# First MLP in six tiles of 512 tokens, with a layer's operands in one part of the memory and the first tile's first two steps in 384 and 128 columns

## The chip, the cores and the metric

The kernel runs on one core of one Trainium2 chip. The metric is the device time of one execution in microseconds, the median of several runs. TensorE (PE in the profile) multiplies, VectorE (DVE) and ScalarE (ACT) work on the results, GpSimd (POOL) is nearly unused, and SyncE (SP) issues the transfers.

## The reference

Attention over chunks of 32 tokens, each with 16 tokens of context on its left and 8 on its right and 8 memory keys, for 4 batches, 8 heads and 768 tokens of head size 64, is followed by two MLPs on the 3,072 tokens of 512 features it yields:

```
for c in range(seq // 32):
    k_full = concat([mem_k, k[max(0, c*32-16) : min(S, c*32+40)]])
    a = exp(s - max(s)) / (sum + 1e-9)      # s = scale * q_c @ k_full.T
    out[c] = a @ v_full
...
h = x @ w_in                                # 512 -> 2048
g = where(h > 0, h, exp(min(h, 0)) - 1)
x = g @ w_out                               # 2048 -> 512
...
h = x @ w_in2
g = s * relu(h)**2 + b
return g @ w_out2                           # 512 features
```

All is fp32. The kernel splits each operand of the MLPs into a high and a low part (fp32r) and makes three matmuls for one product: high x high, high x low, low x high.

## The kernel before, in words

*Attention* goes by 24 units of 128 tokens (six for each batch). A unit has its scores (`psS`, or `psVS` when they share a step with the values of the unit before), a softmax on DVE and ACT (`softmax`, L222 to L237; the first and last unit of a batch also add a mask, L228), transposes of the weights (`step_P`), and the values (`values`, L278, into `psV` or `psVS`). In the units below `NU0` the transposes are four matmuls (`psP`, L251) and a copy on ACT; in the others they are 16 short transposes on DVE (`pt<-sm`, L258). The result of a unit goes straight into `xh` and `xl` for the first two tiles and otherwise by way of DRAM (`x_dram`), from where `load_x` fetches a tile.

*The first MLP* goes by tiles of tokens (`sizes`, eight of three units, 384 tokens) and in each by 16 chunks of 128 hidden features. A step `h1` multiplies a chunk (12 matmuls into `psH`: four blocks of 128 features, three products each; L326 to L328) and makes the activation: two steps on ACT, a sum on DVE (L352), then the high part on ACT and the low one on DVE (`gl`, L184). The step `out1` for the same chunk comes two steps later and adds 12 matmuls into four accumulators `acc`. After a tile's last chunk `put_out` copies the accumulators (L376, L380, L382) into `big`, which goes to `y_dram`.

*The order.* Tile 0's first six chunks come first, then all of tile 1, then the rest of tile 0, then tiles 2 to 7 in order (`seq`). `mlp1_step` gives each half step a share of the attention's remaining steps (`beside`) and of the weights' splitting (`weights_to`; `w<-t`, `t<-raw` on DVE and ACT); the attention is spread over tiles 2, 3 and 4 and ends at tile `TATT` = 5. From there, until tile 7's chunk 8, `prepared` spreads the 160 steps that prepare the second MLP's weights. From tile 7's chunk 10, `load_blocks` fetches what the second MLP starts with. A scheduler decides from that list how each engine's instructions stand, each by its dependences and their priority.

*The second MLP* multiplies blocks of 512 columns in seven products in place of eight (`first_layer`, `second_layer`; `psH<-xc,ws`, `psL<-g2h,ws`), 2,016 matmuls of 512 columns each, with its weight pieces `ws` fetched from DRAM.

*The memory.* Weights of the first MLP lie in two pools, chunks 0 to 7 in one on the right, the others on the left; pools for the second MLP (`xcp`, `wsp`, `yrp`, `ghp`) open on the right where the first eight chunks were, once tile 7 has reached chunk 10 and the pools are closed.

Of the kernel before, what the change touches and what calls it, by code (L numbers as in the profile page):

```python
# [28 lines left out]
NU0 = 6  # L29
HF = 6  # L30
TATT = 5
NFREE = 8
MICRO = 8
HN, NT2 = 512, 3
ORDER = (1, 2, 6, 5, 7, 3, 4)
# [18 lines left out]
def tile_attention_then_two_mlps(ctx, tc, q_in, k_in, v_in, w1, w2, s_in, b_in, out):  # L54
# [22 lines left out]
    def engine(step):  # L77
# [5 lines left out]
    sizes = [3] * 8  # L83
# [8 lines left out]
    early = [ExitStack(), ExitStack()]  # L92
# [10 lines left out]
    ps_v = vctx.enter_context(tc.tile_pool(name="ps_v", bufs=1, space=PSUM))  # L103
    ps_acc = []
# [37 lines left out]
    def split_w(c, i, raw):  # L142

        t = wst.tile([P, DM], I32, tag="t", name="t")
        yield from to_f32(raw, t)
        nm = "io"[i]
        parts = wps[c >= NFREE].tile([P, 2, DM], F32R, tag=f"w{i}_{c}", name=f"w{i}_{c}")
# [183 lines left out]

    def h_mm(t, c, n, xx):
        ps = ps_h.tile([P, 512], F32, tag="h", name="psH")
        for kk in range(KT):
            mm3(ps[:, :n], W["i", c], xx, lambda a: a[:, kk * P:(kk + 1) * P], lambda a: a[:, kk, :n],
                kk == 0, kk == KT - 1)
        return ps
# [20 lines left out]
    def accumulators(t):  # L358
        if not ps_acc:
            vctx.close()  # L360
            ps_acc.append(pctx.enter_context(tc.tile_pool(name="ps_acc", bufs=1, space=PSUM)))
        ACC[t] = [ps_acc[0].tile([P, 512], F32, tag=f"acc{m}", name=f"acc{m}") for m in range(KT)]

    def put_out(t, c, n):
# [6 lines left out]
        if c == NF - 1 or c == HF - 1 and split:  # L371
            for m, acc in enumerate(ACC[t]):
                with tc.high_priority(400):
# [3 lines left out]
                    else:  # L377
                        o = big_tile(n, t >= TATT and m > 0 or m == 3 and t >= 2)
# [145 lines left out]
    ws, used = [], [0]  # L524

    def load_pieces(n):

        while len(ws) < min(n, len(pieces)):
            lay, ii, jj = pieces[len(ws)]
            w = p2["wsp"].tile([P, 2, 2 * P], F32R, tag="ws", name="ws")  # L530
# [12 lines left out]
    def load_blocks(t):  # L543

        t0 = t * 2 * HN
        xc = XC[t] = {j: p2["xcp"].tile([P, 2, 2, HN], F32R, tag=f"xc{j}", name=f"xc{j}") for j in ORDER}
        b12 = p2["yrp"].tile([P, 2, HN], F32, tag="yr", name="b12")
        b11, b21, b22 = (f(xc[j][:, 1]) for j in (1, 2, 3))
# [4 lines left out]
        t3, t2, t4 = (p2["yrp"].tile([P, 2, HN], F32, tag="yr", name=nm) for nm in ("t3", "t2", "t4"))  # L553
# [4 lines left out]
        for j in ORDER:  # L558
            nc.scalar.activation(out=xc[j][:, 0], in_=src[j], func=AF.Copy)
            sub(xc[j][:, 1], src[j], xc[j][:, 0])  # L560
            yield

    def open_second():

        for nm, k, c in (("xcp", 1, ctx), ("wsp", 12, ctx), ("yrp", 4, early[1])):
            p2[nm] = c.enter_context(tc.tile_pool(name=nm, bufs=k, side="right", reuse_waits="tile"))
        p2["blocks"] = load_blocks(0)

    def mlp1_step(t, c):
# [18 lines left out]
        if c == 0 and t == TATT:  # L588
            actx.close()
            op.append(mctx.enter_context(tc.tile_pool(name="op2", bufs=2)))  # L590
            p2["prep"] = early[1].enter_context(tc.tile_pool(name="prep", bufs=2, side="right", reuse_waits="tile"))
# [15 lines left out]
        if t == NTILE1 - 1 and c >= NFREE + 2:  # L607
# [6 lines left out]
    def prepared(t, n):  # L614

        want = min(NPREP * (2 * NF * (t - TATT) + n) // (2 * NF * (NTILE1 - TATT) - 2 * (NF - NFREE)), NPREP)
        while t >= TATT and p2["n"] < want:
# [13 lines left out]
    for slot in seq[-2:]:  # L631
# [6 lines left out]
    early[1].close()  # L638
    g2p, evp, outp, p2["yrp"] = (
        ctx.enter_context(tc.tile_pool(name=nm, bufs=k, reuse_waits="tile"))  # L640
        for nm, k in (("g2p", 4), ("evp", 5), ("outp", 4), ("yrp2", 4)))
    ghp = ctx.enter_context(tc.tile_pool(name="ghp", bufs=3, side="right", reuse_waits="tile"))
# [16 lines left out]
    def first_layer(t, i, g):  # L659

        xc, ii, acc = XC[t], i % 2, {}
        for j in ORDER:
# [4 lines left out]
            for k in range(2):  # L667
                mm3(o, (w[:, 0], w[:, 1]), (xc[j][:, 0], xc[j][:, 1]), lambda a: a[:, k * P:(k + 1) * P],
# [26 lines left out]
    def second_layer(t, gs, beside):  # L695

        keep, acc = {}, {}
        for j in ORDER:
# [4 lines left out]
            for q, g in enumerate(gs):  # L703
                gl, gh = (ghp.tile([P, 2, HN], F32R, tag=nm, name=nm) for nm in ("g2l", "g2h"))
# [99 lines left out]
```

## Time and profile before

| what | value |
|---|---|
| runs | 1091.55, 1089.6, 1096.9 us; median 1091.55 |
| profiled execution, its time and its span | 1094.46 us, 1092.7 us |
| TensorE busy | 1072.1 us (98%), 8,206 matmuls |
| VectorE busy | 783.6 us (72%), 1,299 instructions |
| ScalarE busy | 592.1 us (54%), 939 instructions |
| chain that ended last | PE 82%, DVE 8%, DMA 5%, ACT 3% |
| mean TensorE clock granted | 0.99 |

"Busy" is the time in which at least one instruction of an engine runs; the matmuls overlap, so that a row's mean duration is longer than the distance between two starts. The pace of a run of matmuls is the distance of two starts divided by the number of matmuls between them. In a table of windows the number after x counts the instructions in a window, PEclk is the granted TensorE clock (1.00 is 2.4 GHz, 0.50 is 1.2 GHz), and the DMA share is the mean over the 16 engines.

### The profile page before, as it was taken

Reading aid. Unit: us, or ns where it says so; the run is one execution under the profiler, and the core shown is the slowest. Engines: PE = TensorE matmul, PEld = TensorE weight load, DVE = VectorE, ACT = ScalarE, POOL = GpSimd, SP = SyncE. Lnnn points to the kernel's source line nnn. Section 1 sums busy time; section 2 is a strip of 40 time slices with the busy share of each in tenths; the row PEclk is TensorE's granted clock in tenths of the full one; section 3 lists DMA queues with packets and bytes.
Section 4 is the critical chain, followed back from the end, with each engine's and each line's share of the span. In section 5 each row is a group of like instructions: output and inputs, shape, how many; then the busy total and the mean of one; then the engine's idle time right before and its main releaser. Section 6 shows DMA issues by size and latency. Waiting matters only on the chain.

```text
span 1092.7 us, 20633 instructions
## 1 busy us (share of the span) xinstructions
PE 1072.1 (98%) x8206; PEld 966.0 (88%) x8206; DVE 783.6 (72%) x1299; ACT 592.1 (54%) x939; POOL 0.7 (0%) x6
## 2 busy tenths in 40 slices
PE   7999999999999999999999999999999999999998
PEld 5889999999999999999999987788888788888887
DVE  6899846778678777998884655697356696365854
ACT  4888444334434446787784455754355644255542
POOL 0000000000000000000000000000000000000000
PEclk7899999999999999999999999999999999999999
DMA  8955032433524315898886266777766777766673
GB/s 307 373 221 220 1 109 88 153 102 105 174 81 145 125 40 173 319 335 298 331 326 236 90 187 191 244 210 231 230 191 185 231 214 225 212 197 191 200 204 127
DMA packets 98113, 213.70 MB, mean 196 GB/s; under 512 B 9952, under 2 KB 27360, under 8 KB 95968
## 3 DMA queue, kind: packets, MB, share of 16 engines
q1 hardware_dynamic: 97440, 211.59, 59.4%
q8 instruction: 65, 1.06, 0.4%
q10 hardware_dynamic: 576, 0.79, 0.2%
q14 instruction: 32, 0.26, 0.1%
HBM read 164.89 MB, written 47.45 MB: 194 GB/s over the span
## 4 chain that ended last, share of the span: by engine, by line
PE 82%; DVE 8%; DMA 5%; ACT 3%; issue 1%; SPq 0%; ACTq 0%; DVEq 0%
PE psH L326 14%; PE psH L328 13%; PE psH L327 13%; PE psL L327 7%; PE acc L326 6%; PE psL L328 6%; PE acc L327 6%; PE acc L328 6%; PE psL L326 6%; DVE pt L258 2%; DMA xc<-y_dram 2%; DMA xl<-x_dram 1%; DMA x_dram<-xs 1%; PE psVS L278 1%; PE psVS L219 1%
## 5 line engine op out<-in xcount | busy, mean ns | idle before, releaser
L326 PE MATMUL psH<-xh,w 128*128 128x384 f32 x512 | 175.4, 343 | 2.6 <-ACT pt L180 1.1
L326 PE MATMUL acc<-gh,w 128*128 128x384 f32 x512 | 173.0, 339 | 0.9 <-DVE big L376 0.8
L328 PE MATMUL psH<-xh,w 128*128 128x384 f32 x512 | 173.6, 339 | 0.0
L327 PE MATMUL psH<-xl,w 128*128 128x384 f32 x512 | 173.2, 338 | 0.2 <-DVE xl L184 0.2
L327 PE MATMUL acc<-gl,w 128*128 128x384 f32 x512 | 171.9, 336 | 0.0
L328 PE MATMUL acc<-gh,w 128*128 128x384 f32 x512 | 171.9, 336 | 0.0
L705 ACT ACTIVATE g2h<-g 128x1024 fp32r<-128x1024 f32 x84 | 89.2, 1062 | 89.9 <-PE psL L328 89.6
L327 PE MATMUL psL<-g2l,ws 128*128 128x512 f32 x336 | 131.0, 390 | 1.6 <-DVE g2l L184 1.6
L326 PE MATMUL psH<-xc,ws 128*128 128x512 f32 x336 | 131.8, 397 | 0.6 <-ACT p L656 0.6
L328 PE MATMUL psH<-xc,ws 128*128 128x512 f32 x336 | 131.1, 390 | 0.0
L326 PE MATMUL psL<-g2h,ws 128*128 128x512 f32 x336 | 130.4, 389 | 0.6 <-ACT g2h L705 0.6
L327 PE MATMUL psH<-xc,ws 128*128 128x512 f32 x336 | 130.9, 390 | 0.0
L328 PE MATMUL psL<-g2h,ws 128*128 128x512 f32 x336 | 130.7, 389 | 0.0
L184 DVE TENSOR_TENSOR g2l<-g,g2h 128x1024 fp32r<-128x1024 f32 x84 | 102.2, 1222 | 39.5 <-ACT g2h L705 39.2
L350 ACT ACTIVATE g<-psH 128x384 f32<-128x384 f32 x128 | 62.5, 488 | 113.1 <-PE psH L328 67.0
L180 ACT ACTIVATE gh<-g 128x384 fp32r<-128x384 f32 x128 | 66.9, 522 | 86.8 <-DVE g L352 85.6
L352 DVE SCALAR_TENSOR_TENSOR g<-g,psH 128x384 f32<-128x384 f32 x128 | 70.5, 551 | 49.3 <-ACT g L351 48.4
L326 PEld LDWEIGHTS psH<-xh,w 128*128 128x128 f32 x512 | 97.0, 189 | 5.2 <-ACT pt L180 1.4
L326 PEld LDWEIGHTS acc<-gh,w 128*128 128x128 f32 x512 | 96.6, 189 | 2.4 <-DVE big L376 1.1
L327 PEld LDWEIGHTS psH<-xl,w 128*128 128x128 f32 x512 | 97.1, 190 | 0.5 <-DVE xl L184 0.4
L328 PEld LDWEIGHTS psH<-xh,w 128*128 128x128 f32 x512 | 97.2, 190 | 0.2
L327 PEld LDWEIGHTS acc<-gl,w 128*128 128x128 f32 x512 | 96.2, 188 | 0.3 <-DVE gl L184 0.2
(97 smaller groups left out, 1668.1 us busy)
## 6 DMA issues: line engine op xcount, KB each, us to landing
ws<-s_dram SPq DMA_DIRECT2D x336, 256.0 KB, 2.9
raw<-w SPq DMA_DIRECT2D x64, 512.0 KB, 5.4
s_dram<-right SPq DMA_DIRECT2D x16, 1024.0 KB, 4.5
kb<-k SPq DMA_DIRECT2D x24, 512.0 KB, 5.6
v<-v SPq DMA_DIRECT2D x24, 512.0 KB, 4.3
s_dram<-left SPq DMA_DIRECT2D x16, 768.0 KB, 3.6
q<-q SPq DMA_DIRECT2D x24, 256.0 KB, 5.5
out<-r SPq DMA_DIRECT2D x24, 256.0 KB, 3.5
```

What stands on the lines that cost most here:

```text
L180: return nc.scalar.activation(out=hi, in_=src, func=AF.Copy)
L184: return nc.vector.tensor_tensor(out=lo, in0=src, in1=f(hi), op=ALU.subtract)
L219: mm = nc.tensor.matmul(ps[o, z, r * NCK:(r + 1) * NCK], q[rows, r * U + c * CH:r * U + (c + 1) * CH], kb[rows, r, c * NCK:(c + 1) * NCK], ...
L258: nc.vector.transpose(out=pt[k * CH:(k + 1) * CH, :, rows], in_=sm[rows, :, z, n0:n0 + CH])
L278: nc.tensor.matmul(ps[r % 2 * D:(r % 2 + 1) * D, z, o:o + CH], v[rows, (r * NC + c) * D:(r * NC + c + 1) * D], pt[rows, r, cs], start=True ...
L326: nc.tensor.matmul(o, sa(a[0]), sb(b[0]), start=first, stop=False, skip_group_check=again)
L327: nc.tensor.matmul(o, sa(a[0]), sb(b[1]), start=False, stop=False, skip_group_check=again)
L328: return nc.tensor.matmul(o, sa(a[1]), sb(b[0]), start=False, stop=last, skip_group_check=again)
L350: nc.scalar.activation(out=g[:, :n], in_=ps[:, :n], func=AF.Relu, scale=-1.0)
L352: nc.vector.scalar_tensor_tensor(out=g[:, :n], in0=g[:, :n], scalar=-1.0, in1=ps[:, :n], op0=ALU.add, op1=ALU.max)
L705: nc.scalar.activation(out=gh, in_=g[:, block], func=AF.Copy)
```

## The change

The tiles have four units, 512 tokens, six in all. The first two tiles take eight units, so `NU0` is 8. Chunks 0 and 1 of tile 0 are multiplied in two parts: in 384 columns (`psE`) as soon as three units (`NEARLY`) are done and in 128 columns after the fourth. The attention's last step comes at `ATT_END`, tile 3, chunk 8; the second MLP's weights are prepared from there on until the last tile's chunk 10. The weights of the first layer of the first MLP and the tiles `xh`, `xl` lie on the right; later their memory holds the weight pieces, the blocks `xc` and the parts `g2h`, `g2l` of the second MLP. Those of the second layer lie on the left.

```
-    sizes = [3] * 8
+    sizes = [4] * 6
-NU0 = 6
-TATT = 5
-NFREE = 8
+NU0 = 8
+NEARLY = 3
+ATT_END = (3, 8)
+NBLOCK = 10
...
-    wps = [early[0].enter_context(tc.tile_pool(name="wpa", bufs=1, side="right")),
-           mctx.enter_context(tc.tile_pool(name="wpb", bufs=1))]
+    wps = [ctx.enter_context(tc.tile_pool(name="wpi", bufs=1, side="right")),
+           mctx.enter_context(tc.tile_pool(name="wpo", bufs=1))]
-    xp = mctx.enter_context(tc.tile_pool(name="xp", bufs=1))
+    xp = ctx.enter_context(tc.tile_pool(name="xp", bufs=1, side="right"))
...
+    EARLY = {}
+    def h_part(ps, c, xx, lo, hi):
+        for kk in range(KT):
+            mm3(ps[:, lo:hi], W["i", c], xx, lambda a: a[:, kk * P:(kk + 1) * P], lambda a: a[:, kk, lo:hi],
+                kk == 0, kk == KT - 1)
+    def h_early(c):
+        EARLY[c] = ps_e.tile([P, 512], F32, tag="e", name="psE")
+        h_part(EARLY[c], c, X[0], 0, NEARLY * U)
     def h_mm(t, c, n, xx):
+        if t == 0 and c in EARLY:
+            ps = EARLY.pop(c)
+            h_part(ps, c, xx, NEARLY * U, n)
+            return ps
...
-        elif 1 < t < TATT:
-            a0, total, k, ks = ready[2], len(steps) - ready[2], NF * (t - 2) + c, NF * (TATT - 2)
+        elif t > 1 and (t, c) < ATT_END:
+            a0, total, k, ks = ready[2], len(steps) - ready[2], NF * (t - 2) + c, NF * (ATT_END[0] - 2) + ATT_END[1]
...
-        want = min(NPREP * (2 * NF * (t - TATT) + n) // (2 * NF * (NTILE1 - TATT) - 2 * (NF - NFREE)), NPREP)
+        begin = 2 * (NF * ATT_END[0] + ATT_END[1])
+        want = min(NPREP * (2 * NF * t + n - begin) // (2 * NF * (NTILE1 - 1) + 2 * NBLOCK - 2 - begin), NPREP)
...
+    def high(c):
+        return wps[0].tile([P, 2, HN], F32R, tag=f"w0_{c}", name=f"hi{c}")
     def open_second():
-        for nm, k, c in (("xcp", 1, ctx), ("wsp", 12, ctx), ("yrp", 4, early[1])):
-            p2[nm] = c.enter_context(tc.tile_pool(name=nm, bufs=k, side="right", reuse_waits="tile"))
+        z = (NTILE1 + 1) % 2
+        halves = iter(range(10))
+        for j in (1, 2, 3, 6, 5, 7, 4):
+            if j in (6, 5):
+                xc = xp.tile([P, 2, 2, HN], F32R, tag=f"{'xh' if j == 6 else 'xl'}{z}", name=f"xc{j}")
+                XC[j] = xc[:, 0], xc[:, 1]
+            else:
+                XC[j] = high(next(halves)), high(next(halves))
```

TensorE's order at the first tile, before, once the fourth unit's scores are issued. `xh`, `xl` are the tile's two parts, `w_0` and `w_1` weights; the rows name the source's line:

```order
L219 MATMUL psS<-kb,q 32x64 x32
L326 MATMUL psH<-xh,w_0_382 128x384
L327 MATMUL psH<-xl,w_0_382 128x384
L328 MATMUL psH<-xh,w_0_382 128x384
L326 MATMUL psH<-xh,w_0_382 128x384
L327 MATMUL psH<-xl,w_0_382 128x384
L328 MATMUL psH<-xh,w_0_382 128x384
L326 MATMUL psH<-xh,w_0_382 128x384
L327 MATMUL psH<-xl,w_0_382 128x384
```

And after, from the fourth unit's values on (the 384 columns, `psE`, stand before this piece):

```order
L279 MATMUL psV<-pt,v 64x32 x32
L220 MATMUL psS<-kb,q 32x64 x32
L327 MATMUL psE<-xh,w_0_436 128x128
L252 MATMUL psP<-ident,sm_106 128x128 x3
L328 MATMUL psE<-xl,w_0_436 128x128
L329 MATMUL psE<-xh,w_0_436 128x128
```

The tile's first products, which were whole once three units were done, are now whole only when the fourth unit's values are.

VectorE's chain of one unit's softmax and transposes, before; `gl` and `g` are the low part and the sum of the MLP's activation:

```order
L231 TENSOR_REDUCE nmx<-psVS 128x8
L232 TENSOR_TENSOR sm_103<-psVS,nmx 128x2x4x64
L234 TENSOR_REDUCE sums<-sm_103 128x8
L235 TENSOR_SCALAR rs<-sums 128x8
L236 RECIPROCAL rs<-rs 128x8
L237 TENSOR_TENSOR sm_103<-sm_103,rs 128x2x4x64
L258 STREAM_TRANSPOSE pt<-sm_103 32x4x32 x4
L352 SCALAR_TENSOR_TENSOR g<-g,psH 128x384
L258 STREAM_TRANSPOSE pt<-sm_103 32x4x32 x4
L184 TENSOR_TENSOR gl<-g,gh 128x384
L258 STREAM_TRANSPOSE pt<-sm_103 32x4x32 x8
```

And of unit 9 after the change:

```order
L232 TENSOR_REDUCE nmx<-psVS 128x8
L233 TENSOR_TENSOR sm_107<-psVS,nmx 128x2x4x64
L235 TENSOR_REDUCE sums<-sm_107 128x8
L236 TENSOR_SCALAR rs<-sums 128x8
L237 RECIPROCAL rs<-rs 128x8
L238 TENSOR_TENSOR sm_107<-sm_107,rs 128x2x4x64
L394 COPY big<-acc_1429 128x512
L366 SCALAR_TENSOR_TENSOR g<-g,psH 128x512
L259 STREAM_TRANSPOSE pt<-sm_107 32x4x32 x4
L185 TENSOR_TENSOR gl<-g,gh 128x512
L394 COPY big<-acc_1431 128x512
L259 STREAM_TRANSPOSE pt<-sm_107 32x4x32 x12
```

Two copies of the output (`big<-acc`) stand between that unit's softmax and its last transposes.

TensorE after the change, where unit 10's values are computed; they stand in two parts with two matmuls between:

```order
L329 MATMUL psH<-xh,w_10_1537 128x512
L279 MATMUL psVS<-pt,v 64x32 x13
L327 MATMUL acc_2204<-gh,w_8_1425 128x512
L328 MATMUL acc_2204<-gl,w_8_1425 128x512
L279 MATMUL psVS<-pt,v 64x32 x19
L220 MATMUL psVS<-kb,q 32x64 x32
L329 MATMUL acc_2204<-gh,w_8_1425 128x512
```

Between the start of a unit's chain and its values stand 48 matmuls of the MLP for most units (36 to 120 in all), where before it was 60 to 84 from tile 2 on.

## Rows read from the trace of the kernel before

**Rows 1.** Windows (us; busy time of each engine, count, PEclk, DMA share, GB/s).

```profile
40.00:60.00 20.00, 18.90 (x323) 16.13 (x322) 19.57 (x36) 18.92 (x36) 0.00 (x0) 1.00 0.93 360
...
79.00:80.00 1.00, 1.00 (x4) 1.00 (x4) 1.00 (x3) 0.60 (x2) 0.00 (x0) 0.50 1.05 343
...
440.00:500.00 60.00, 60.00 (x347) 60.00 (x347) 55.04 (x105) 48.52 (x92) 0.00 (x0) 1.00 0.89 326
...
880.00:1080.00 200.00, 200.00 (x879) 163.92 (x878) 129.53 (x124) 94.79 (x106) 0.00 (x0) 1.00 0.71 205
```

**Rows 2.** TensorE's timeline, end of the first MLP (start, duration, line, work).

```profile
619.75 0.33 PE L326 MATMUL acc<-gh,w 128*128 128x384 f32 x1
...
623.21 0.34 PE L328 MATMUL acc<-gh,w 128*128 128x384 f32 x1
623.38 0.39 PE L326 MATMUL psH<-xc,ws 128*128 128x512 f32 x1
```

**Rows 3.** TensorE's timeline, end of the second MLP.

```profile
1079.71 0.39 PE L328 MATMUL psL<-g2h,ws 128*128 128x512 f32 x1
...
1088.55 0.39 PE L328 MATMUL psL<-g2h,ws 128*128 128x512 f32 x1
```

**Rows 4.** TensorE's timeline, first stage; brackets hold idle time before.

```profile
28.67 0.69 PE L326 MATMUL psH<-xh,w 128*128 128x384 f32 x1
...
36.87 0.32 PE L278 MATMUL psV<-pt,v 64*64 64x32 f32 x8
...
40.47 0.27 PE L251 MATMUL psP<-ident,sm 128*128 128x128 f32 x1
...
40.75 0.34 PE L326 MATMUL psH<-xh,w 128*128 128x384 f32 x1
...
74.74 0.30 PE L278 MATMUL psVS<-pt,v 64*64 64x32 f32 x2 [0.93 <-DVE pt L258]
75.40 0.32 PE L278 MATMUL psVS<-pt,v 64*64 64x32 f32 x8 [0.36 <-DVE pt L258]
...
79.70 0.52 PE L328 MATMUL psH<-xh,w 128*128 128x384 f32 x1
80.02 0.52 PE L326 MATMUL acc<-gh,w 128*128 128x384 f32 x1
```

**Rows 5.** VectorE's timeline, first and ninth sum of the activation.

```profile
34.07 0.56 DVE L352 SCALAR_TENSOR_TENSOR g<-g,psH 128x384 f32<-128x384 f32 x1 [1.87 <-ACT g L351]
...
80.45 0.56 DVE L352 SCALAR_TENSOR_TENSOR g<-g,psH 128x384 f32<-128x384 f32 x1
```

**Rows 6.** TensorE's timeline, two units' values and the scores between.

```profile
153.27 1.13 PE L278 MATMUL psVS<-pt,v 64*64 64x32 f32 x64
154.34 0.86 PE L219 MATMUL psVS<-kb,q 64*32 64x64 f32 x64
...
165.77 1.52 PE L278 MATMUL psVS<-pt,v 64*64 64x32 f32 x64
```

**Rows 7.** VectorE's timeline, the same unit's first and last instructions.

```profile
156.09 0.69 DVE L231 TENSOR_REDUCE nmx<-psVS 128x8 f32<-128x512 f32 x1
...
163.88 2.58 DVE L258 STREAM_TRANSPOSE pt<-sm 32x128 f32<-32x128 f32 x8
```

**Rows 8.** Groups by line, form (busy us, mean ns; idle before).

```profile
L184 DVE TENSOR_TENSOR gl<-g,gh 128x384 fp32r<-128x384 f32 x128 | 71.1, 556 | 27.2 <-ACT gh L180 26.5
L352 DVE SCALAR_TENSOR_TENSOR g<-g,psH 128x384 f32<-128x384 f32 x128 | 70.5, 551 | 49.3 <-ACT g L351 48.4
...
L184 DVE TENSOR_TENSOR w<-t,w 128x512 fp32r<-128x512 f32 x32 | 21.8, 687 | 0.2
...
L380 DVE COPY big<-acc 128x384 f32<-128x384 f32 x16 | 8.7, 550 | 4.3 <-PE acc L328 4.0 <-DMA y_dram<-big 0.3
```

**Rows 9.** Waits of TensorE (us in total, times, longest).

```profile
PE psVS L278 <- DVE pt L258: 2.6, 6, 0.9
```

**Rows 10.** DMA issues of the page (KB each, median us to landing).

```profile
ws<-s_dram SPq DMA_DIRECT2D x336, 256.0 KB, 2.9
```

More of the change, by code (lines that the diff above doesn't have):

```diff
@@ L146, in split_w @@
         nm = "io"[i]
-        parts = wps[c >= NFREE].tile([P, 2, DM], F32R, tag=f"w{i}_{c}", name=f"w{i}_{c}")
+        parts = wps[i].tile([P, 2, DM], F32R, tag=f"w{i}_{c}", name=f"w{i}_{c}")
         hi, lo = parts[:, 0], parts[:, 1]
@@ L504, in weights_to @@
             wnext[0] += 1
+    first = next(k for k, g in enumerate(steps) if g[0] == (step_V, NEARLY - 1))
     for n_, s in enumerate(steps[:ready[0]]):
@@ L529, in load_pieces @@
             lay, ii, jj = pieces[len(ws)]
-            w = p2["wsp"].tile([P, 2, 2 * P], F32R, tag="ws", name="ws")
+            n = len(ws) % 12
+            if len(ws) < 12 and n % 2 == 0:
+                p2["ws"] += [high(10 + n // 2)]
+            w = p2["ws"][n // 2].rearrange("p z (j n) -> p (z j) n", j=2)[:, 2 * (n % 2):2 * (n % 2) + 2]
             nc.sync.dma_start(out=f(w), in_=s_dram[lay, ii, :, PIECE[jj]])
@@ L587, in mlp1_step @@
             wt = [(w1, max(n0 + (MICRO * NF - n0) * (2 * c + z) // 28, MICRO * (c + z)), 4) for z in (1, 2)]
-        if c == 0 and t == TATT:
+        if (t, c) == ATT_END:
             actx.close()
             op.append(mctx.enter_context(tc.tile_pool(name="op2", bufs=2)))
-            p2["prep"] = early[1].enter_context(tc.tile_pool(name="prep", bufs=2, side="right", reuse_waits="tile"))
+            p2["prep"] = mctx.enter_context(tc.tile_pool(name="prep", bufs=2, reuse_waits="tile"))
             p2["steps"] = prepare_all()
@@ L596, in mlp1_step @@
             weights_to(w1, MICRO * (c + 1), 4)
-        if t == NTILE1 - 1 and c == NFREE + 2:
-            early[1].close()
-            early[0].close()
+        if t == NTILE1 - 1 and c == NBLOCK:
             open_second()
@@ L636, in tile_attention_then_two_mlps @@
     mctx.close()
[L638 to L642, printed above, removed]
+    g2p, evp, outp, yrp, ghp = (
+        ctx.enter_context(tc.tile_pool(name=nm, bufs=k, reuse_waits="tile", side=side))
+        for nm, k, side in (("g2p", 4, "left"), ("evp", 5, "left"), ("outp", 4, "left"), ("yrp", 1, "left"),
+                            ("ghp", 1, "right")))
+    p2["yr"] = [yrp.tile([P, 2, HN], F32, tag=f"yr{k}", name=f"yr{k}") for k in range(4)]
+    z = NTILE1 % 2
+    gls = [ghp.tile([P, 2, HN], F32R, tag=f"g2l{k}", name=f"g2l{k}") for k in range(2)]
+    for nm in ("xh", "xl"):
+        pair = xp.tile([P, 2, 2, HN], F32R, tag=f"{nm}{z}", name=f"g2{nm}")
+        gls += [pair[:, 0], pair[:, 1]]
+    ghs, gls, ngh = gls[3:], gls[:3], [0]
     psp = ctx.enter_context(tc.tile_pool(name="psp", bufs=8, space=PSUM, reuse_waits="tile"))
@@ L703, in second_layer @@
             for q, g in enumerate(gs):
-                gl, gh = (ghp.tile([P, 2, HN], F32R, tag=nm, name=nm) for nm in ("g2l", "g2h"))
+                gl, gh = gls[ngh[0] % 3], ghs[ngh[0] % 3]
+                ngh[0] += 1
                 nc.scalar.activation(out=gh, in_=g[:, block], func=AF.Copy)
```

43 lines of the change are left out of this document (23 added, 20 removed).

## The prediction

> **What bounds the kernel now.** I read the page first. TensorE is busy in 98 of 100 parts of the span, in nearly every slice, and the chain that ended last lies on it for 82 parts; so time is to be had from the matmuls' own pace, or from the few places where TensorE stands or runs at half clock. The table of windows then says which stage is which [rows 1]: in the stretch from 440 to 500 us, deep in the first MLP, and in the one from 880 to 1080 us, in the second, TensorE has no idle time and the full clock; only in the window from 40 to 60 us is it below that, and there VectorE (DVE) is busy 19.57 of 20 us. In the one from 79 to 80 us DVE is busy throughout and TensorE's granted clock is 0.50, the lower of its two levels, while it is 1.00 from 40 to 60 us; TensorE had stood idle twice for DVE before it fell.
>
> TensorE's own timeline at the end of each MLP gives its pace. From 619.75 to 623.21 us there are 20 matmuls of 384 columns, 3.46 us, so 0.1730 us each [rows 2]; from 1079.71 to 1088.55 us there are 39 of 512 columns, 8.84 us, so 0.2267 us each [rows 3]. The window of 200 us gives 0.2275 (200/879) and that of 60 us 0.1729 (60/347) [rows 1]. The durations in a row are longer than the pace, since matmuls overlap; only starts count.
>
> **The change, part by part.**
>
> *Matmuls of the first MLP.* Before there are 16 chunks x 8 tiles x 24 = 3,072 of 384 columns: x 0.1730 = 531.5 us. After there are 2,280 of 512 columns (0.2268: 517.1 us), 24 of 384 (4.15 us) and 24 of 128. The last kind has no row; the nearest is the transposes with 128 columns: from 40.47 to 40.75 us one transpose and one matmul of 384 columns start, 0.28 us, less 0.173, so 0.11 [rows 4]. Below, the line through 0.1730 and 0.2267 gives 0.065 at 128 columns; above, it is no dearer than 384 columns, 0.173. I take 0.11, 2.6 us (1.6 to 4.2). Together 523.9: **-7.6 us** (-6.0 with 0.2275; -8.6 with the cheap narrow ones). The Trainium skill ("TensorE: Matmul & The Clock Gate", section "Back-to-back issue gap") gives an isolated gap of N/2.4 + 2.5 ns at the fast clock; by that, as an estimate, 162.5 and 215.8 ns, 499.2 and 497.3 us, a gain of 1.9 instead of 7.6 and a sum of +1.5 instead of -4.2. The rows differ from it: they show 13 ns over N/2.4 at both widths, so each matmul that is saved gives back more than that rule has it.
>
> *Transposes.* Units 6 and 7 are transposed on TensorE now: 8 x 0.11 = **+0.9**. In exchange DVE has 32 short transposes fewer.
>
> *The first stage.* It runs from the first matmul at 28.67 us to the start of the first tile's third sum while the second tile's first products are made, at 80.02 us [rows 4]: 51.35 us. In it TensorE has 180 matmuls (31.1 us at 0.173) and some 7.4 us of attention (three units at 2.3 us: scores 0.8, values 1.07, four transposes; and the start of a fourth); 12.85 us are lost, in waits for DVE (0.93 and 0.36 us at 74.74 and 75.40 among them) and at half clock (0.32 us from 79.70 to 80.02 for one matmul of 384 columns). On DVE the first sum of an activation comes at 34.07 and the ninth at 80.45, 46.4 us for 45.0 us of work by the order and the rows' durations [rows 5]. After the change the same nine are of 512 columns, but fewer weight parts and transposes lie between: 44.0 us of work by the order of DVE. The first one comes later, since it needs the fourth unit: that unit's values at 36.9 in the trace, then the copy, 24 narrow matmuls and the activation, some 43.5 us. Then DVE would be through at 43.5 + 44.0 x 46.4/45.0 = 88.9 and TensorE at the same place at 88.5, with 53.3 us of own work (156 wide x 0.2268, the 6.75 us of the narrow ones, 11.2 us of attention for five units in place of three), so 6.5 lost instead of 12.85. That is the best, -6.3. The worst is that as much is lost as before, 0. Since DVE waited only 1.4 of its 46.4 us I take a value near the first end: **-5.0**. The DMA engines are 93% busy there [rows 1] and two more units (2.5 MB) are fetched ahead; DVE's work covers that. If it did not, the first weights would come late, which lies inside the same bounds.
>
> *The attention beside the MLP.* From one unit's scores to its values TensorE does MLP matmuls while DVE does the softmax and 16 transposes. The unit whose scores end at 155.20 shows this chain [rows 6, 7]: its last transposes end at 166.46, 11.26 us later, one sum and one difference of 0.56 us in between, its values start at 165.77, and take 1.52 us instead of 1.07 (153.27 to 154.34), so about 0.45 is lost. There 60 matmuls stood between, 10.4 us. With 512 columns sum and difference take 0.69 instead of 0.55 (as the weight's difference of that width) and the chain is 11.52 [rows 8]. The order after has 48 matmuls there for most units, 10.9 us and 0.19 for the turn; a unit loses 11.52 - 11.08 - 0.25 = 0.2, where 0.25 is by how much the values may start ahead. A mask or a copy of the output (0.55 us at 384 columns, 0.69 at 512, and a turn) in the chain adds 0.72 each. By the order: unit 9 has two copies (1.6), unit 10 only 38 matmuls (2.0), unit 11 a mask and 46 (1.4), unit 13 four sums of the output (2.6), unit 14 has 47 (0.4), unit 17 a mask and a difference (1.6), unit 23 a mask (0.9), six others 0.2 each: 11.7 us. Units 10 and 13 have their values in two parts with matmuls between; I take half for these, 9.4. Before, with 60 to 84 in between, the waits of values for the transposes are 2.6 us in six places, of which 1.29 lie in the first stage, and 0.45 of the stretched values: 1.9 [rows 9]. **+7.5**, bounds 0 (DVE early everywhere) and +12.1 (14 us, when copies ahead of a chain delay units 17 and 21 too).
>
> *The rest, at nothing.* The second MLP's matmuls are in the same order. Its weight preparation starts half a tile earlier in a tile of other length; DVE is 92% busy in the stretch from 440 to 500 us [rows 1], and the new table gives it 2.42 of 160 steps per half step of 2.73 us where it had 2 per 2.08: 8% fewer per us, so TensorE's matmuls cover it as they do now; uncovered, a step late by its own 0.69 us now and then would cost a few us. Its operands lie where weights were, and the last weight there is read 36 matmuls, 8.2 us, before the second MLP's first one; a piece lands in 2.9 us [rows 10]. If all twelve pieces came one behind the other at the end it would cost about 2 us.
>
> Sum: -7.6 + 0.9 - 5.0 + 7.5 = -4.2. The profiled execution took 1094.46 us, 2.9 over the median of 1091.55; it would give 1090.3, and the median 1087.4.
>
> **Rivals.** *A, the chain stays hidden.* The order of a scheduler need not cost what the single row says: DVE may run ahead, as in the units before the change whose values don't wait. Then the waits are 3 us in place of 9.4: 1.1 net, the sum -10.6, time 1081. For it: before, with 72 to 84 matmuls there, values wait in a handful of places only. Against: 48 x 0.2268 is 10.9 us, and the unit of before with 10.4 us had the loss.
>
> *B, slower: DVE is the bound.* The same chain in units 9 to 23, with copies and masks, costs 14 us, and the first stage, full of DVE's work, loses as much as before: -7.6 + 0.9 + 0 + 12.1 = +5.4, time 1097. It decides where the chain exceeds the matmuls by some 0.75 us in each of 15 units. For it: 19.57 of 20 us busy, and the four sums of unit 13. Against: DVE has less work in total (32 transposes less, and fewer, wider instructions).
>
> *C, no gain of width.* The 512 columns in this stage go in proportion, 0.173 x 512/384 = 0.2307 us: 526.0 + 6.75 us, +1.3 in place of -7.6; the sum is +4.7, time 1096. Against it stand both ends of the MLPs, with the same kind of matmul. The page named above leads there in part only, to 1093.
>
> **Numbers.** Forecast 0.50, A 0.27, B 0.18, C 0.05. The likeliest is 1087.4. With the ends of the terms the best is -8.6 + 0.9 - 6.3 - 1.9 = -15.9 and the worst -4.4 + 0.9 + 0 + 12.1 = +8.6; without a tenth at each end 1078 to 1098. 1% (about what a measurement of this kernel tells from no change) is 1080.6 and 1102.5: of A four tenths and of the forecast's lower end a little lie below, 0.16; of B and C a few lie above, 0.05; between them 0.79.
>
> **What the profile after would show.** TensorE's starts 0.227 us apart in the stretch where before they were 0.173; VectorE's ninth sum at about 89 us and the half clock near 78 us gone; rows of values waiting for transposes of some 9 us in sum, longest at units 9 to 13 with 1 to 2.6 us. If the starts are 0.23 apart, C holds; if the waits are under 4 us, A; if the waits are above 12 and DVE is full in the first stage with a mark beyond 94 us, B. A second MLP that takes longer than before by more than 1 us, or starts with a gap, would make the part at nothing wrong.

## The result and the profile after

The changed kernel takes 1100.41 us (median of 11 runs) and the kernel before 1092.91 us (11 runs): ratio 1.0074, 95% interval 1.0058 to 1.0091. It is slower, by 7.5 us; the forecast was 1087.4, with a range up to 1098. The profiled execution took 1099.46 us with a span of 1097.1 us, 4.4 over the span of before; the readings below are of this pair of profiles, which lies closer together than the medians do.

The page's line on TensorE looks the same as before, 98% busy:

```profile
span 1097.1 us, 18847 instructions
...
PE 1073.1 (98%) x7470; PEld 871.7 (79%) x7470; DVE 768.2 (70%) x1199; ACT 577.8 (53%) x839; POOL 0.7 (0%) x6
```

The windows of the changed kernel (columns as in [rows 1]) say more:

```profile
40.00:60.00 20.00, 18.16 (x313) 14.63 (x313) 17.93 (x33) 17.98 (x35) 0.00 (x0) 0.83 0.99 371
...
360.00:380.00 20.00, 18.62 (x186) 14.85 (x185) 14.65 (x35) 6.69 (x11) 0.00 (x0) 0.83 0.42 120
...
440.00:500.00 60.00, 60.00 (x263) 49.13 (x262) 50.81 (x88) 44.81 (x75) 0.00 (x0) 1.00 0.85 303
500.00:560.00 60.00, 60.00 (x263) 49.07 (x262) 52.62 (x92) 46.27 (x78) 0.00 (x0) 1.00 0.90 324
...
880.00:1080.00 200.00, 200.00 (x878) 163.95 (x877) 130.72 (x124) 94.98 (x107) 0.00 (x0) 1.00 0.73 208
```

In 120 us of the first MLP without attention there are 526 matmuls of 512 columns, 0.2281 us each, where the forecast had 0.2268; and from 360 to 380 us there is a new stretch at half clock. The half clock near 78 us [rows 1] is gone, as forecast, but the window from 40 to 60 us, at full clock before, now has a mean of 0.83. The starts on TensorE's timeline give the pace more exactly: one group of the first layer, 12 matmuls, from 500.57 to 503.32.

```profile
500.57 0.39 PE L327 MATMUL psH<-xh,w 128*128 128x512 f32 x1
...
503.32 0.39 PE L327 MATMUL acc<-gh,w 128*128 128x512 f32 x1
```

That is 2.75 us for 12. Over 35 steady steps from 422 to 618 us a step of 24 takes 5.507 us (0.2294 each), with hardly any spread; the same reckoning gives 4.168 us for 24 of 384 columns before (0.1737, against 0.1730 at the very end, [rows 2]). The second MLP's pace is unchanged: 878 matmuls in the 200 us in which it had 879.

The waits of values for DVE's transposes are 6.1 us in 16 places (before 2.6 in 6, [rows 9]). The greatest loss, in several pieces, is at unit 21. TensorE's timeline there:

```profile
368.21 0.61 PE L279 MATMUL psVS<-pt,v 64*64 64x32 f32 x16
369.15 0.30 PE L279 MATMUL psVS<-pt,v 64*64 64x32 f32 x2 [0.33 <-DVE pt L259]
369.81 0.31 PE L279 MATMUL psVS<-pt,v 64*64 64x32 f32 x6 [0.35 <-DVE pt L259]
370.46 0.30 PE L279 MATMUL psVS<-pt,v 64*64 64x32 f32 x2 [0.34 <-DVE pt L259]
371.11 1.28 PE L279 MATMUL psVS<-pt,v 64*64 64x32 f32 x38 [0.36 <-DVE pt L259]
372.33 1.18 PE L220 MATMUL psVS<-kb,q 64*32 64x64 f32 x64
373.44 0.80 PE L327 MATMUL psH<-xh,w 128*128 128x512 f32 x1
374.03 0.63 PE L328 MATMUL psH<-xl,w 128*128 128x512 f32 x1
374.46 0.63 PE L329 MATMUL psH<-xh,w 128*128 128x512 f32 x1
```

The values take 4.12 us instead of 1.07, 3.05 lost in pieces between transposes, and the matmuls behind them come 0.43 us apart instead of 0.23: half clock (the window's mean of 0.83 makes 6.8 us at 0.50), for nine matmuls, some 2.1 us lost with the scores. On VectorE one instruction stands ahead of that unit's softmax, the low part of the next tile, 2.29 us long, and VectorE stands idle 0.92 us for it: it needs the high part `xh`, and ScalarE has just waited for the fetched tile (ScalarE and then VectorE):

```profile
355.94 1.91 ACT L303 ACTIVATE xh<-xl 128x2048 fp32r<-128x2048 f32 x1 [1.69 <-DMA xl<-x_dram]
```

```profile
357.88 2.29 DVE L185 TENSOR_TENSOR xl<-xl,xh 128x2048 fp32r<-128x2048 f32 x1 [0.92 <-ACT xh L303]
```

Idle time and instruction make 3.2 us, about what the unit loses. Unit 17 has the same in front of it:

```profile
298.68 2.29 DVE L185 TENSOR_TENSOR xl<-xl,xh 128x2048 fp32r<-128x2048 f32 x1 [1.08 <-ACT xh L303]
```

Summed in this way (a unit's values less 1.07 us), units 9 to 23 lose 12.7 us: 0.9, 1.9, 1.0, 0, 1.1, 0.1, 0.6, 0.6, 2.8 (unit 17), 0, 0, 0, 3.05 (unit 21), 0, 0.7. In the kernel before the same sum, with unit 8, which loses nothing after, is 2.7 us.

The first stage's mark, the start of the seventh group of sums, answers to 80.02 in [rows 4]; the first and ninth sum on VectorE to [rows 5]; and the second MLP starts at 627.16 instead of 623.38 [rows 2]:

```profile
91.01 0.39 PE L327 MATMUL acc<-gh,w 128*128 128x512 f32 x1
...
627.16 0.39 PE L327 MATMUL psH<-hi,hi 128*128 128x512 f32 x1
```

```profile
43.10 0.68 DVE L366 SCALAR_TENSOR_TENSOR g<-g,psE 128x512 f32<-128x512 f32 x1
...
94.89 0.68 DVE L366 SCALAR_TENSOR_TENSOR g<-g,psH 128x512 f32<-128x512 f32 x1
```

### The profile page after: what moved, and what is told of

Its sections match the earlier page's. It is cut to its first block, busy times and chain, and to the rows that moved or that the text cites. A ratio compares the mean times of both kernels' runs of the same rounds, so it can differ in the third digit from the quotient of the medians.

```text
span 1097.1 us, 18847 instructions
## 1 busy us (share of the span) xinstructions
PE 1073.1 (98%) x7470; PEld 871.7 (79%) x7470; DVE 768.2 (70%) x1199; ACT 577.8 (53%) x839; POOL 0.7 (0%) x6
## 4 chain that ended last, share of the span: by engine, by line
PE 83%; DVE 9%; DMA 4%; ACT 2%; issue 1%; SPq 0%; DVEq 0%; ACTq 0%
PE psH L327 13%; PE psH L329 13%; PE psH L328 13%; PE acc L327 7%; PE psL L328 7%; PE acc L328 6%; PE psL L329 6%; PE acc L329 6%; PE psL L327 6%; DVE pt L259 3%; DMA hi<-y_dram 1%; PE psV L279 1%; DMA xl<-x_dram 1%; DMA x_dram<-xs 1%; PE psVS L279 1%
## 5 line engine op out<-in xcount | busy, mean ns | idle before, releaser
L327 PE MATMUL acc<-gh,w 128*128 128x512 f32 x384 | 151.6, 395 | 1.1 <-DVE big L390 1.1
L328 PE MATMUL acc<-gl,w 128*128 128x512 f32 x384 | 150.7, 392 | 0.0
L327 PE MATMUL psH<-xh,w 128*128 128x512 f32 x376 | 150.4, 400 | 0.0
L329 PE MATMUL acc<-gh,w 128*128 128x512 f32 x384 | 150.3, 392 | 0.0
L329 PE MATMUL psH<-xh,w 128*128 128x512 f32 x376 | 149.1, 397 | 0.0
L328 PE MATMUL psH<-xl,w 128*128 128x512 f32 x376 | 147.5, 392 | 0.0
L366 DVE SCALAR_TENSOR_TENSOR g<-g,psH 128x512 f32<-128x512 f32 x94 | 64.4, 685 | 73.0 <-ACT g L365 72.3
L327 PE MATMUL psH<-hi,hi 128*128 128x512 f32 x240 | 93.7, 397 | 0.9 <-ACT p L694 0.9
L329 PE MATMUL psH<-hi,hi 128*128 128x512 f32 x240 | 93.6, 390 | 0.0
L328 PE MATMUL psH<-hi,hi 128*128 128x512 f32 x240 | 93.6, 390 | 0.0
L328 PE MATMUL psL<-g2l,hi 128*128 128x512 f32 x224 | 87.4, 390 | 2.8 <-DVE g2l L185 2.8
L329 PE MATMUL psL<-g2xl,hi 128*128 128x512 f32 x224 | 87.2, 389 | 0.0
L327 PE MATMUL psL<-g2xl,hi 128*128 128x512 f32 x224 | 87.0, 390 | 0.0
L185 DVE TENSOR_TENSOR gl<-g,gh 128x512 fp32r<-128x512 f32 x96 | 66.2, 690 | 27.4 <-ACT gh L181 26.4
L329 PEld LDWEIGHTS psH<-xh,w 128*128 128x128 f32 x376 | 71.2, 189 | 16.5
```

Source lines behind the costliest of these rows:

```text
L185: return nc.vector.tensor_tensor(out=lo, in0=src, in1=f(hi), op=ALU.subtract)
L327: nc.tensor.matmul(o, sa(a[0]), sb(b[0]), start=first, stop=False, skip_group_check=again)
L328: nc.tensor.matmul(o, sa(a[0]), sb(b[1]), start=False, stop=False, skip_group_check=again)
L329: return nc.tensor.matmul(o, sa(a[1]), sb(b[0]), start=False, stop=last, skip_group_check=again)
L366: nc.vector.scalar_tensor_tensor(out=g[:, :n], in0=g[:, :n], scalar=-1.0, in1=ps[:, :n], op0=ALU.add, op1=ALU.max)
```

## The experiments

Ratios are to the kernel before in the same series, with their interval. "Loss" is that of the units' values as above.

**Where do the waits of the values come from?**

```
e1:  -  if m % 2:                     e7:  -  sub(xl, f(xl), xh)
     +  if m % 2 and t < 1:                +  nc.gpsimd.tensor_tensor(out=xl, in0=f(xl), in1=f(xh), op=ALU.subtract)
e9:  -  nc.scalar.activation(out=xh, in_=f(xl), func=AF.Copy)
     -  sub(xl, f(xl), xh)
     +  for k in range(KT):
     +      nc.scalar.activation(out=xh[:, k], in_=f(xl)[:, k], func=AF.Copy)
     +      sub(xl[:, k], f(xl)[:, k], xh[:, k])
```

e1, copies by ScalarE:

> The changed kernel, all copies of an output tile on ScalarE instead of half of them on VectorE, from tile 1 on. Theory (the softmax chain on VectorE is the wait, and each VectorE instruction put into it lengthens it): the loss at unit 9's values falls from 0.9 to about 0.2 us; units 17 and 21, whose chain is held up by the 2.29 us difference of the next tile's xl rather than by copies, keep 2.8 and 3.0. Total about -1 us against the changed kernel. Rival (the copies are what delays unit 21, and its 3 us of waits bring the stretch of half clock after it): unit 21's waits fall under 1 us, no half clock at 371 us, total -4 to -5 us.

1100.93 us, ratio 1.0082 (1.0064 to 1.0100). Unit 9 lost 0 us instead of 0.9: without its two copies the chain is short enough. Unit 21 lost 2.1, unit 17 3.5, and half clock followed both; the expected microsecond in the total is not seen. So the copies are a part, and not the part that decides.

e7, the low part on GpSimd:

> The changed kernel with the low part of a fetched tile (xl, 128x2048, four times) made on GpSimd instead of VectorE. Theory: that 2.29 us instruction stands ahead of the softmax of units 17 and 21 and is what makes their values wait longest; without it they lose about 1 us together instead of 5.8, and the half clock that follows unit 21 goes (2 us): total -6 to -7 us against the changed kernel. Rival (it does not matter what stands in front; the copies or the 48 matmuls do): units 17 and 21 keep over 4 us together, total within 2 us.

1106.24 us, ratio 1.0131 (1.0111 to 1.0150), both expected totals missed. Units 17 and 21 lost 5.7 and 5.2 us. The timelines show why, GpSimd first and then VectorE:

```profile
301.82 4.62 POOL L304 TENSOR_TENSOR xl<-xl,xh 128x2048 fp32r<-128x2048 f32 x1 [69.77 <-ACT xh L303]
```

```profile
302.92 0.69 DVE L366 SCALAR_TENSOR_TENSOR g<-g,psH 128x512 f32<-128x512 f32 x1 [2.95 <-ACT g L365]
304.31 2.68 DVE L185 TENSOR_TENSOR gl<-g,gh 128x512 fp32r<-128x512 f32 x1 [0.70 <-PE acc L328]
306.92 0.68 DVE L229 TENSOR_TENSOR sm<-psVS,cmask 128x512 f32<-128x512 f32 x1
```

The difference `gl`, with both inputs in SBUF, takes 2.68 us instead of 0.69: it ends at 306.99, some 0.55 us after GpSimd (306.44), as if it had run only then; the sum before it, with one input in PSUM, is not slowed. The Trainium skill has the rule ("GPSIMD Engine Reference", section "Specifications"): GpSimd's interfaces to SBUF are shared with VectorE, with contention where a VectorE instruction has two SBUF inputs; the trace agrees. So VectorE is not relieved. It is held up by the sum's wait too, 2.95 us for ScalarE's `g`, which stands behind `xh` in ScalarE's order: to take `xl` off VectorE leaves the wait for the fetched tile as it was.

e9, the low part in four parts:

> The changed kernel with xh and xl of a fetched tile made in four parts of 512 columns instead of one instruction of 2048 each. Theory (one 2.29 us instruction ahead of the softmax is what delays units 17 and 21): the softmax's steps get between the parts; their losses fall from 5.8 to 2 to 3 us, and the half clock after unit 21 goes: total -4 to -6 us against the changed kernel. Rival: VectorE's order keeps the four parts together (2.8 us), and nothing changes or it is 1 us worse.

1098.50 us, ratio 1.0068 (1.0040 to 1.0096): unit 17 lost 4.5, unit 21 2.2 us, 13.3 in all. The rival holds: at unit 17 the four parts stand together, 2.50 us behind 1.04 us of idle time. No run moved the fetch of the tile alone, so how the loss at these units divides between the wait for `xh` and `xl` itself is not shown.

e3, all transposes on TensorE:

```
-        if u < NU0:        (in step_P)          "pt": ("a", "a", "-", "a", "v")
+        if u < NU:                              "pt": ("a", "a", "-", "a", "a")
```

> The changed kernel with all units' transposes on TensorE (4 matmuls each and a copy on ScalarE) instead of 16 short ones on VectorE from unit 8 on. Theory: the chain on VectorE loses 5.1 us and gains 0.6 on ScalarE, so no unit waits as before (-12.7 and -2 for the half clock), TensorE has 64 transposes more at 0.11 (+7.0): total -6 to -8 us against the changed kernel. Rival (the transposes are a wait of their own, once for the softmax and once for the copy, and take a PSUM buffer of the MLP's): waits at the transposes of 0.5 to 1 us per unit eat it, total -2 to +8.

1102.45 us, ratio 1.0092 (1.0067 to 1.0117). From unit 9 on no values wait for their transposes any more (one wait of 2.7 us for a sum of the MLP stands in the middle of unit 12's), but TensorE has 64 transposes more, and they now wait for the softmax:

```profile
PE psP L252 <- DVE sm L238: 6.6, 6, 3.0
```

3.0 and 1.8 us of it are at units 17 and 21 again. With e1, e7 and e9: whatever was taken out of the chain, what stands ahead of it at these units stayed, and TensorE's next instruction of the attention waited in its place.

e2, more matmuls between values:

```
-ATT_END = (3, 8)
+ATT_END = (3, 12)
```

> The changed kernel, attention ends at tile 3, chunk 12 instead of 8. Theory (chain of 11.5 us against 48 matmuls, 11.1 us): from tile 2 on there are 60 matmuls, 13.8 us, between most units' values, so these values no longer wait; what is left are units 9 to 11 (about 4 us); the losses of values go from 12.7 to 4 to 6 us and the half clock in the attention's stretch goes (2 us): total -8 to -10 us against the changed kernel, about 1.000 of the kernel before. The preparation of the second MLP's weights becomes 14% denser; if VectorE can't hide it, TensorE shows waits after 420 us and half of the gain is lost (rival).

1090.16 us, ratio 0.9983 (0.9970 to 0.9995); 10.2 us under the changed kernel by the medians of the two series, 8.4 by the two profiles. The loss is 6.0 us instead of 12.7, there is no half clock near 370 us, and from 420 us on the steps keep 5.51 us: the denser preparation is hidden. The wait rows, 6.1 us in the changed kernel, read 2.8:

```profile
PE psVS L279 <- DVE pt L259: 2.8, 7, 0.8
```

So the theory of the chain holds, by its cure: twelve more matmuls between two values, 2.75 us.

**Is the first stage worth anything?** e4 takes the split of the first two steps away:

```
-        if n_ in (first, first + 2):
-            h_early((n_ - first) // 2)
```

> The changed kernel without the split of the first tile's first two steps (both in 512 columns after the fourth unit). If TensorE's own work sets the first stage, the 24 matmuls of 384 columns that ran beside the fourth unit's softmax (6.4 us of TensorE's time at partly half clock) move behind it and the narrow ones go: +3 to +6 us against the changed kernel. Rival: VectorE, full in that stage, sets its end; the first two sums come later by what the matmuls take (1.5 us each more), and the total changes by 0 to +2.

1100.78 us, ratio 1.0081 (1.0057 to 1.0104), 0.4 us over the changed kernel: the rival. TensorE's first matmul of the MLP comes at 34.69 instead of 28.02 and the second MLP at 627.80 instead of 627.16. The 6.7 us of head start are waited off later: VectorE's ninth sum comes at 94.55 where the changed kernel has it at 94.89. VectorE sets this stage; between its first and its ninth sum it is busy 49.67 of 51.79 us in the changed kernel (columns as in [rows 1]):

```profile
43.10:94.89 51.79, 51.79 (x599) 41.50 (x595) 49.67 (x96) 47.87 (x89) 0.00 (x0) 0.94 0.81 298
```

**Why do matmuls of 512 columns take 0.2294 us here and 0.2267 in the second MLP?** e10 takes the activation away in tile 4, e8 makes groups of 24 there (both shortened). These two, e6, e11 and e12 ran once each and are read for the pace of a step alone:

```
e10: +  if t == 4 and c > 1:                     e8: +  if t == 4 and c % 2 == 0:
     +      G[1, t, c] = G4[c % 2]                   +      next(parts) ... continue
     +      return                                   +  if t == 4: ... out1(*seq[n_ - 3]) ...
```

> The changed kernel; in tile 4 the activation of chunks 2 to 15 is left out (the second layer multiplies the parts of chunks 0 and 1 again). It asks why 24 matmuls of 512 columns take 5.51 us in the first MLP and 5.44 in the second. Theory (the activation's reads of psH and the waits for gh and gl disturb TensorE): in tile 4 the 24 take 5.44. Rival (it lies in TensorE's own alternation of groups, 12 into psH and 12 into the accumulators, or in the operands): they keep 5.51. The time as a whole is not of interest.

Steps in tile 4 stay at 5.50 to 5.51 us: it is not the activation.

> The changed kernel; in tile 4 two chunks' first layers follow each other and then two second layers, so that groups are of 24 matmuls instead of 12. If each change between the layers' groups costs TensorE 33 ns (both theories), 48 matmuls take 10.95 us in place of 11.01; if the excess is in each group of 12 whatever precedes it, 11.01.

48 matmuls take 10.95 us. A change between the layers' groups costs, at 33 ns, and not the group as such.

e5 has the new placement alone, in tiles of 384 tokens (and NU0 = 6, ATT_END = (5, 0), no split, x allocated at 512 tokens):

```
-    sizes = [4] * 6
+    sizes = [3] * 8
```

> The new placement of the operands alone: tiles of 384 tokens, six units transposed on TensorE, attention to the end of tile 4, no split, as before. Theory: the placement has no part in the result: 24 matmuls of 384 columns take 4.167 us as before and the time is that of the kernel before within 2 us; it may add the 1.2 us by which the second MLP's waits for g2l are longer in the changed kernel. Rival (operands in one part of the memory slow TensorE's reads): 24 matmuls take 4.22 us or more, +5 us.

1096.22 us, ratio 1.0033 (1.0020 to 1.0046), 4.213 us for 24 in place of 4.168: in 60 us there are 343 matmuls instead of 347 [rows 1], and the rival holds nearly to its number.

```profile
440.00:500.00 60.00, 60.00 (x343) 60.00 (x343) 55.09 (x105) 48.52 (x92) 0.00 (x0) 1.00 0.89 327
```

e6, e11 and e12 ask what of the placement it is:

```
e6:  -  xp = ctx.enter_context(tc.tile_pool(name="xp", bufs=1, side="right"))    (opened after wpi)
     +  xp = ctx.enter_context(tc.tile_pool(name="xp", bufs=1))                  (opened first, left)
e11: -  mctx.enter_context(tc.tile_pool(name="wpo", bufs=1))
     +  mctx.enter_context(tc.tile_pool(name="wpo", bufs=1, side="right"))       (behind xp)
e12 (kernel before): +  dynamic_dma_scratch_size=1024
```

> The changed kernel with the tiles xh and xl on the left side of the memory, so that both steps' streamed operands (x and g) lie there, as in the kernel before; weights stay where they are (first layer right, second left). The steady step of 24 matmuls of 512 columns takes 5.51 us in the changed kernel, 1.2% over the second MLP's pace (5.44); the placement alone cost as much in 384 columns (4.21 against 4.17). Theory X (the streamed operands' place changes with every group): 5.44 to 5.45. Theory W (the weights' side changes with every group): still 5.51.

> The changed kernel with both layers' weights and x on the right side, g's parts on the left. Theory W (the weights' side changes with every group of 12): 24 matmuls take 5.44 to 5.45 us. Theory X (the streamed operand's side does): still 5.51, since x is right and g left.

> The kernel before with nothing but the scratch memory of the DMA rings cut to 1024 bytes, as the change has it; it shifts every operand by 15 KB down on the left. Theory X or W: 24 matmuls of 384 columns keep 4.167 us. Rival S (the shift of addresses, not the side, is the cause): 4.21.

e12 keeps 4.168 us: not the scratch memory. e6 and e11 came out at 5.527 and 5.547 us, above what either theory gave (the executions took 1109.09 and 1104.59 us), and the two layers part. In e6 the first layer's 12 take 2.79 us and the second's 2.73; in e11 2.74 and 2.80 (TensorE's timelines, e6 and then e11):

```profile
520.50 0.39 PE L327 MATMUL psH<-xh,w 128*128 128x512 f32 x1
...
523.29 0.39 PE L327 MATMUL acc<-gh,w 128*128 128x512 f32 x1
...
526.02 0.39 PE L327 MATMUL psH<-xh,w 128*128 128x512 f32 x1
```

```profile
523.28 0.39 PE L327 MATMUL psH<-xh,w 128*128 128x512 f32 x1
...
526.02 0.40 PE L327 MATMUL acc<-gh,w 128*128 128x512 f32 x1
...
528.82 0.39 PE L327 MATMUL psH<-xh,w 128*128 128x512 f32 x1
```

Where the operands begin in memory (the built program's addresses) orders these: on the right they begin 32 bytes past a multiple of 64, on the left at a multiple. In the slowest groups streamed operand and weights differ in this (e6: x left, weights right; e11: g left, weights right). In the changed kernel they agree inside a group, but one layer lies on the right and the other on the left. Both theories by side had missed it; the next two runs move one side by 32 bytes.

```
p_left8:  +  pad = ctx.enter_context(tc.tile_pool(name="pad", bufs=1, side="left"))    (p_right8: side="right")
          +  pad.tile([P, 8], F32, tag="pad", name="pad")                              (ahead of all other tiles)
```

> The changed kernel with 32 bytes put in front of everything on the left side of the memory, nothing else. In the changed kernel the operands on the right begin 32 bytes past a multiple of 64 and those on the left at a multiple of 64. The slowest groups of the runs so far (2.79 us with x left, 2.80 us with the weights right) are those whose streamed operand and weights differ in this. Theory A (operands of neighbouring groups should agree in it): all begin at 32 now, as in the second MLP, and 24 matmuls take 5.44 to 5.45 us instead of 5.51, in all -5 to -6 us. Rival (it is the side or the distance, not the alignment): 5.51.

> The changed kernel with 32 bytes at the far end of the right side, so that all operands begin at multiples of 64. Theory A: 24 matmuls take 5.44 to 5.45 us, -5 to -6 us, and the second MLP keeps its pace. Rival: 5.51.

5.440 us in both, in every step; the second MLP keeps its pace. 1095.21 and 1097.98 us in one run each, 5.2 and 2.4 under the changed kernel; the second total is less than was expected, and one run doesn't tell more. The windows of p_left8, 533 matmuls in the 120 us that held 526, and one group of 12 in 2.72 us:

```profile
440.00:500.00 60.00, 60.00 (x266) 49.70 (x265) 51.25 (x88) 45.04 (x76) 0.00 (x0) 1.00 0.85 304
500.00:560.00 60.00, 60.00 (x267) 49.69 (x266) 54.08 (x95) 47.56 (x81) 0.00 (x0) 1.00 0.91 337
```

```profile
502.13 0.39 PE L329 MATMUL acc<-gh,w 128*128 128x512 f32 x1
...
504.85 0.39 PE L329 MATMUL psH<-xh,w 128*128 128x512 f32 x1
```

The same 32 bytes in tiles of 384 tokens:

> The new placement alone in tiles of 384 tokens, with the 32 bytes on the left. Without them it took 4.213 us for 24 matmuls and 1.0033 of the kernel before. Theory A (the placement's cost is the alignment): 4.16 us or a little less, total 5.5 to 6.5 us less: 0.997 to 0.999 of the kernel before. Rival (in 384 columns it is something else of the placement): 4.21 and 1.003.

4.160 us, 1092.39 us, ratio 1.0000 (0.9991 to 1.0010): what the placement cost is gone with the shift, also where nothing else is changed.

The kernel before shows the effect on a small scale. Its x and g begin at a multiple of 64; eight chunks have weights at a multiple and eight have them 32 bytes past one. Groups of 12 take 2.08 us with either half of the weights. Only at each change between the halves, where the groups of the two layers alternate between them, six groups take up to 2.10:

```profile
442.08 0.34 PE L326 MATMUL acc<-gh,w 128*128 128x384 f32 x1
...
444.16 0.34 PE L326 MATMUL psH<-xh,w 128*128 128x384 f32 x1
...
452.48 0.35 PE L326 MATMUL psH<-xh,w 128*128 128x384 f32 x1
...
454.58 0.34 PE L326 MATMUL acc<-gh,w 128*128 128x384 f32 x1
```

So at 384 columns a change of the remainder costs, and a lasting difference between weights and streamed operand does not. At 512 columns the lasting difference costs too. At the end of the first MLP three groups of the second layer follow each other. In e11 (g left, weights right) these 36 matmuls take 8.40 us, 0.2333 each up to the last one; in the changed kernel (both left) 8.20, from 618.96 to 627.16, with only the first five starts further apart than 0.227:

```profile
625.86 0.40 PE L327 MATMUL acc<-gh,w 128*128 128x512 f32 x1
...
634.26 0.39 PE L327 MATMUL psH<-hi,hi 128*128 128x512 f32 x1
```

**Do the two causes make up the miss?** b1 has ATT_END = (3, 12), the copies of e1, and the attention beside tile 0's rest over one chunk more; b2 adds the 32 bytes on the left:

```
-  ... min(c - HF, NF - HF - 4), NF - HF - 3       -  if c == NF - 4 and 1 <= ...
+  ... min(c - HF, NF - HF - 3), NF - HF - 2       +  if c == NF - 4 + (t == 0) and 1 <= ...
```

> The changed kernel with three edits against the values' waits: attention to tile 3, chunk 12, all output copies from tile 1 on by ScalarE, and the attention beside the rest of tile 0 spread over one chunk more (its tile's fetch one chunk later). Theory: of the 6.0 us that the first of these alone left, units 9 and 10 lose 1.3 + 2.4 less 1 us: total 2 to 4 us under that run, 0.995 of the kernel before. Rival: tile 2 now comes late from DRAM, TensorE waits for it, and nothing is gained.

1087.64 us, ratio 0.9943 (0.9923 to 0.9963), loss 3.45 us, 12.8 us under the changed kernel.

> The three edits against the values' waits and the 32 bytes on the left together. If the two causes are independent: 24 matmuls take 5.44 us, 95 steady steps of 24 gain 0.067 us each, 6.3 us under the run with the three edits alone (1087.6): 1081.3, 0.989 of the kernel before. Rival (faster matmuls leave VectorE's chain less time, 0.13 us per unit, and the waits come back): 1084.

1082.29 us, ratio 0.9903 (0.9886 to 0.9919), 5.44 us a step, loss 3.7 us. It is 5.4 us under b1, where 6.3 were expected of independent causes; the expected 0.989 lies in the interval, the waits did not come back, and so the causes add as far as these runs tell. It beats both kernels, by 10.4 us and 18.1 us.

## Why the prediction was wrong, step by step

| term | forecast | measured (profiled pair) |
|---|---|---|
| matmuls of the first MLP | -7.6 | 95 x 5.507 + 6.9 - 128 x 4.168 = -3.4 |
| transposes on TensorE | +0.9 | 22 narrow ones in 2.38 us, 0.11 each: +0.9 |
| first stage | -5.0, a mark at 89.8 | mark at 91.0: -3.8 |
| values' waits | +7.5 (9.4 for 1.9) | +10.0 (12.7 for 2.7) |
| other delays of the MLP's matmuls behind the mark | 0 | 6.8 for 6.6: +0.2 |
| second MLP | 0 | 465.8 for 465.2: +0.6 |
| sum | -4.2 | +4.5; the spans differ by +4.4 |

The row of other delays is what the distances from a matmul of the first MLP to whatever starts next have over the steady pace, summed from the mark to the second MLP. The half clock after unit 21 is in it with some 2 us of the 6.8, but in the kernel before other delays of this kind were greater (the turns to and from the attention, the end of the half clock near 78 us, groups at a change of the weights' half). The slower pace inside the first stage, about 0.4, is in two rows. Of the 8.6 us between forecast and these spans the matmuls are 4.2 and the values' waits 2.5.

*The matmuls.* This step failed. The width does give what the row of the second MLP said, once the operands are aligned: 5.44 us for 24 is 0.2267 each (p_left8); as the kernel stood it was 0.2294. But 0.2267 was read from the second MLP and carried to the first across a change of placement that was in the diff, and "its operands lie where weights were" was costed for transfers only. The trace of before had only a trace of it, the groups of 2.10 us among those of 2.08, which I did not look for; what it did show is that one stage's pace is a fact of that stage. The forecast took 0.1730 from the last 20 matmuls besides, where the steady step has 0.1737 (533.5 us in all for 531.5). Rival C, no gain of width, came near the pace (0.2307) for a wrong reason: the loss is per change of group, and present at 384 columns too (e5). The Trainium skill's isolated gap ("TensorE: Matmul & The Clock Gate", section "Back-to-back issue gap") gave -1.9 for this term, by luck not far from -3.4: its two paces, 162.5 and 215.8 ns, stand in no row before or after.

*The values' waits.* The mechanism was right (chain against 48 matmuls, e2), the size too small by 2.5 us net, in units 17 and 21: 2.8 and 3.05 us for 1.6 and 0.2. The order of VectorE showed `xl` (2.29 us at this width) ahead of their softmax; I put delays of these two units into the upper bound only, as copies ahead of a chain, and the idle time before `xl`, 1.08 and 0.92 us, nowhere. Unit 10 lost 1.9, what the order gave before I halved it; unit 13's half, 1.3, was close to its 1.1.

*The half clock.* It was priced in the first stage, where [rows 1] showed it, and nowhere as a consequence of a wait that the change makes. Here 3 us of broken work was followed by 6.8 us at 0.50, about 2 us lost, and with the waits gone (e2, b1) that stretch is gone. Not every such wait has it: the 2.8 us lost at unit 17 in the same execution were followed by none.

*The first stage.* VectorE's first sum was forecast for 43.5 and came at 43.10; the ninth was forecast for about 89 and came at 94.89. The forecast had 44.0 us of VectorE's work between them by the order; the trace has 49.67 in 51.79 us. So VectorE is the bound, as the forecast had it, but its work was counted too small, and the split bought nothing (e4).

Rival B, slower, came nearest as to the waits: they were 12.7 where it had 14; its first stage (no gain) did not come about, and the misplaced operands took that part instead. Its time, 1097, being nearest to 1100.41 is in part luck.

## What to carry to other kernels

A pace read in one stage holds for the operands of that stage: when a change moves operands, look at the addresses that the build gives for what is streamed, the weights and the neighbouring group (here they differed by 32 bytes modulo 64), and try a pad of 32 bytes before anything else is concluded. When a wider tile makes each unit of side work wait for fewer matmuls, list what stands ahead of the softmax on VectorE for each unit, the long ones first; giving the attention four more chunks was worth 8 to 10 us, shortening the chain alone (e1, e3, e7, e9) nothing that a total showed.

## What the runs showed of the hardware

- TensorE's matmuls of 512 columns take 0.2267 us where all operands of neighbouring groups begin at the same remainder modulo 64 bytes (0 or 32, both tried: p_right8, p_left8), 0.2294 where the two layers differ (the changed kernel), and 0.2328 to 0.2335 (2.79 and 2.80 us for 12: e6, e11) in groups whose weights and streamed operand differ; in e11 that lasts through 36 matmuls without a change. In 384 columns the two layers' difference costs 4.213 against 4.160 us for 24 (e5, e13), while groups of the kernel before whose weights differ from what is streamed take 2.08 us like the others, save at a change. Why the two widths part in this was not found, nor what in TensorE's reads does it. Only distances of 32 bytes were tried, and the addresses of the two sides differ by 32 modulo 128 and 256 as well, so that 64 is not told from these.
- A GpSimd instruction of 4.62 us on SBUF held up a VectorE instruction with two SBUF inputs that started under it: 2.68 us instead of 0.69, with its end some 0.55 us behind GpSimd's (e7).
